# A fixed instruction order exchanged for another, with w_in's low parts made by TensorE, single VectorE steps and a split accumulator

## The chip, the cores and the metric

The kernel runs on one core of a Trainium2 chip. Its engines are TensorE (PE; PEld is its weight load), VectorE (DVE), ScalarE (ACT), GpSimd (POOL) and SyncE (SP), which here issues the loads and stores. The metric is the device time of one execution in microseconds (us).

## The reference

A gated linear attention (4 batches, 8 heads, 768 steps, head size 48) feeds a feed-forward layer (3072 tokens, 384 to 2048 to 384).

```python
for t in range(S):
    state = alpha[:, :, t, :, None] * state + np.einsum('bhd,bhe->bhde', k[:, :, t], v[:, :, t])
    y[:, :, t] = np.einsum('bhd,bhde->bhe', q[:, :, t], state)
x = np.ascontiguousarray(y.transpose(0, 2, 1, 3)).reshape(B * S, H * D)
h = x @ w_in
sp = np.maximum(h, 0.0) + np.log1p(np.exp(-np.abs(h)))
g = h * erf(sp)
return (g @ w_out).astype(np.float32)
```

The weights arrive as 64-bit floats; q, k, v and alpha as 32-bit floats.

## The kernel before

**Attention** goes in 24 chunks (2 pairs of batches, 12 chunks of 64 steps). A chunk n has these steps, each a method of `Chunk`: loads `la lk lq lv` (SP); `sb`, a scan over alpha backwards with the reciprocal of its segment ends and their copy into `start`, and `sa`, the scan forwards (DVE); `kk`, `qq`, the scaled K and Q (DVE); `pn`, four transposes of K (PE), and `kn`, their eviction (ACT); `td`, the decayed state (DVE); `qt`, `ps`, `sv`, `pu`, small matrix products that occupy parts of the PE array (lines 333 to 384), named by their outputs py, pS, py and pu; `mk`, the causal mask (DVE); `ta`, the new state (DVE); `xh` (ACT) and `xl` (DVE), the output split into a high part and a rest.

**The feed-forward layer** goes in 12 block rows (0 to 11) of 256 tokens (two chunks each), a block row in 4 groups g of 512 hidden features, a group in two halves. Steps, methods of `Moe`: `hm`, 18 matmuls of 128x256 (three products of high and low parts over three K tiles) into `ph`; `he`, its eviction to `hs` (ACT); `u`, tanh (ACT); `n1`, `n2`, `n3`, two logarithms and an exponential (ACT); `m1`, two chained DVE steps (t from s and w, then w from t and w); `g`, a Gelu (ACT); `z1`, `z2` (DVE); per half `ga`, the high part gh (ACT), `gl`, the rest gl (DVE), and `om`, 18 matmuls into the accumulator `acc`; at the end of a block row `oe` (ACT) and `od` (SP), three outputs each. `u` and `g` need another ACT table set than `n1` to `n3`; `need` loads it where it changes (line 225). A *block* below means one `hm` or one `om`: 192 in all; a *block row* is the 256 tokens that share an accumulator.

**The weights** come in 12 chunks of w_in (`wli` loads, n = 3g + K tile) and 16 of w_out (`wlo`). Each is turned into 32-bit floats by `wy` (ACT), `wv` and `wz` (DVE: a shift, then two chained bitwise steps on `wbuf`), then split: `wh` the high part (ACT), `wq` the low part (DVE subtract). Group g of `hm` needs chunks 3g to 3g + 2 of w_in.

**The order** is one table, ORDER (line 26): step names in sequence. Each instruction of PE, DVE, ACT and SP is issued through a `Queue` (line 168) that ties it to the one before it on its engine, so every engine works strictly in the table's order and waits where its next step isn't ready. All of them have line 176 in the profile. Behind the table come eight small DVE steps and one matmul that test whether values stayed in range, and a branch to a general version that isn't taken.

Of the kernel before, what the change touches and what calls it, by code (L numbers as in the profile page):

```python
# [10 lines left out]
F32 = mybir.dt.float32  # L11
# [8 lines left out]
RMAX = 1e30  # L20
# [6 lines left out]
wli_5 wyi_5 wvi_5 la_0 sb_0 wzi_5 whi_5 sa_0 wli_9 wyi_9 lk_0 kk_0 pn_0 wqi_5 kn_0 wvi_9 lq_0 qq_0 ps_0 wzi_9  # L27
mk_0 wli_8 wyi_8 wvi_8 lv_0 sv_0 whi_9 wqi_9 la_1 wlo_7 wzi_8 wli_1 wli_2 sb_1 whi_8 wqi_8 sa_1 wli_4 wyi_2
wvi_2 xh_0 lk_1 xl_0 wyi_1 wzi_2 whi_2 wlo_0 wlo_6 wvi_1 wli_0 pu_0 ta_0 lq_1 wzi_1 td_1 la_2 whi_1 wyi_4 qq_1
kk_1 wqi_2 pn_1 kn_1 wvi_4 lk_2 wlo_3 qt_1 ps_1 wli_3 wqi_1 sb_2 wzi_4 whi_4 sa_2 mk_1 wyi_0 wvi_0 kk_2 wyo_7  # L30
wvo_7 lv_1 wlo_1 sv_1 xh_1 wzi_0 whi_0 wzo_7 pu_1 ta_1 wyo_1 wqi_4 wli_7 wyi_7 wvo_1 xl_1 wqi_0 pn_2 td_2 wvi_7
wli_11 who_7 wzo_1 wzi_7 wyi_3 lv_2 wvi_3 wqo_7 wzi_3 hm_0_0_0 he_0_0_0 hm_0_0_1 lq_2 wyo_0 wvo_0 qq_2 wli_6
lk_3 who_1 wqo_1 he_0_0_1 wli_10 u_0_0 wzo_0 who_0 la_3 sb_3 wyo_6 wlo_4 wvo_6 sa_3 kn_2 qt_2 wzo_6 whi_3 whi_7
wqi_7 n1_0_0 wyi_6 wqi_3 wyo_3 ps_2 mk_2 wlo_2 wqo_0 sv_2 wvi_6 n2_0_0 n3_0_0 xh_2 hm_0_1_0 he_0_1_0 wvo_3 who_6
pu_2 wzi_6 whi_6 kk_3 lv_3 m1_0_0 g_0_0 wqo_6 hm_0_1_1 wzo_3 wqi_6 ta_2 z1_0_0 wyi_10 wvi_10 z2_0_0 he_0_1_1
hm_0_2_0 he_0_2_0 wyi_11 xl_2 pn_3 kn_3 wzi_10 wvi_11 wlo_15 who_3 wqo_3 td_3 lq_3 qq_3 lk_4 wlo_5 whi_10 wzi_11
wqi_10 wyo_4 wvo_4 hm_0_2_1 wlo_8 qt_3 ps_3 whi_11 mk_3 wyo_2 wvo_2 sv_3 wqi_11 hm_0_3_0 lv_5 he_0_2_1 ga_0_0_0
wlo_11 gl_0_0_0 wyo_15 wvo_15 u_0_2 wzo_4 xh_3 xl_3 u_0_1 wzo_15 ga_0_0_1 gl_0_0_1 wzo_2 he_0_3_0 who_4 wqo_4
who_15 la_4 sb_4 n1_0_2 pu_3 ta_3 wyo_5 wqo_15 hm_1_0_0 he_1_0_0 n1_0_1 hm_0_3_1 he_0_3_1 wvo_5 kk_4 who_2 wzo_5
om_0_0_0 n2_0_1 n3_0_1 lv_4 hm_1_2_0 lq_4 he_1_2_0 sa_4 wqo_2 pn_4 om_0_0_1 qq_4 td_4 qt_4 n2_0_2 wyo_8 m1_0_1  # L40
wvo_8 n3_0_2 m1_0_2 g_0_1 wlo_9 hm_1_3_0 he_1_3_0 z1_0_1 g_0_2 wzo_8 z2_0_1 z1_0_2 kn_4 hm_1_0_1 he_1_0_1 who_5
wqo_5 lq_5 la_5 ga_0_1_1 gl_0_1_1 ga_0_1_0 gl_0_1_0 wlo_10 z2_0_2 hm_1_3_1 he_1_3_1 wyo_10 wvo_10 wyo_11 wvo_11
who_8 wyo_9 wvo_9 hm_1_2_1 ps_4 wqo_8 wlo_14 wlo_12 lk_5 hm_1_1_0 u_0_3 he_1_2_1 om_0_1_0 mk_4 wzo_11 pu_4 u_1_0
n1_1_0 wzo_9 sv_4 who_11 wzo_10 sb_5 om_0_1_1 who_10 wqo_10 who_9 sa_5 hm_1_1_1 xh_4 xl_4 ta_4 wyo_14 n1_0_3
kk_5 n2_0_3 wvo_14 pn_5 td_5 qq_5 n3_0_3 ga_0_2_1 gl_0_2_1 qt_5 wqo_11 om_0_2_1 kn_5 m1_0_3 u_1_2 wzo_14 wlo_13
wyo_12 ps_5 mk_5 sv_5 pu_5 wqo_9 ga_0_2_0 gl_0_2_0 om_0_2_0 he_1_1_0 wvo_12 lk_6 he_1_1_1 who_14 g_0_3 z1_0_3
wyo_13 lq_6 la_6 xh_5 xl_5 u_1_1 n1_1_1 z2_0_3 ga_0_3_0 wzo_12 who_12 wqo_14 ga_0_3_1 sb_6 hm_2_0_0 he_2_0_0
n2_1_0 gl_0_3_1 hm_2_2_0 he_2_2_0 gl_0_3_0 wvo_13 n3_1_0 n1_1_2 ta_5 hm_2_0_1 hm_2_3_0 wzo_13 om_0_3_1 who_13
n2_1_2 he_2_0_1 m1_1_0 n3_1_2 g_1_0 he_2_3_0 lv_6 wqo_13 u_2_0 wqo_12 om_0_3_0 lv_7 oe_0_1 od_0_1 hm_2_2_1 kk_6
m1_1_2 g_1_2 oe_0_2 z1_1_0 pn_6 sa_6 he_2_2_1 kn_6 la_7 hm_2_3_1 z2_1_0 ga_1_0_1 ga_1_0_0 oe_0_0 qq_6 lk_7 td_6  # L50
# [36 lines left out]
u_7_0 m1_6_1 lk_17 gl_5_2_1 la_17 gl_5_2_0 u_6_3 pn_16 qt_16 kn_16 he_7_2_0 om_5_2_1 om_5_2_0 ga_6_0_1 m1_6_2
# [44 lines left out]
def gla_moe(ctx: ExitStack, tc: tile.TileContext, q, k, v, alpha, w_in, w_out, out):  # L132
# [652 lines left out]
```

## Time and profile before

| | us |
|---|---|
| median of 3 runs (lowest, highest) | 566.34 (564.23, 567.69) |
| the profiled execution | 565.46 |
| its span, first to last instruction | 563.7 |
| PE busy / DVE busy / ACT busy | 512.1 / 487.3 / 472.3 |
| last accumulator matmul ends | 556.3 |

Busy time counts an instruction's own record. Records of one engine overlap a little where the next needn't wait: the start-to-start distance in a full queue, called the *slot* below, is shorter than the record. A matmul's record is longer still than its slot.

### The profile page before, as it was taken

To read this page: it belongs to the slowest core of one execution; us is meant where nothing else is said; L and a number is where in the kernel's file an instruction comes from. 1 tells how busy PE (TensorE), PEld (TensorE's weight loads), DVE (VectorE), ACT (ScalarE), POOL (GpSimd) and SP (SyncE) were. 2 spreads that over 40 slices of the span, in tenths; PEclk is the share of its full clock that TensorE was granted. 3 is DMA by queue.
4 is the path that set the end of the run, shared out by engine and by line. 5 is a ranking of instruction groups with operands and counts; after the bars stand their busy time and mean duration, and the time that the engine had idled before them with its cause. 6 is when DMAs were issued, how large, how long until landed. Compare 5 with 4: busy or idle time off the path is not lost.

```text
span 563.7 us, 17947 instructions
## 1 busy us (share of the span) xinstructions
PE 512.1 (91%) x7962; PEld 491.4 (87%) x7962; DVE 487.3 (86%) x649; ACT 472.3 (84%) x644; POOL 3.5 (1%) x18
## 2 busy tenths in 40 slices
PE   0255899989999999999999999999999999999894
PEld 0245789989999999999999999999999999999884
DVE  6899999999989999979698798989787988676972
ACT  2337799989999999999988979989988998999961
POOL 2000000000000000000000000000000000000000
PEclk9998989989999999999999999999999999999988
DMA  6986232321302221113103112113110111000001
GB/s 182 279 266 189 91 104 86 91 63 54 82 15 68 72 49 48 59 30 99 28 10 110 34 44 76 31 42 102 44 57 22 49 49 44 2 10 20 2 29 34
DMA packets 38101, 38.98 MB, mean 69 GB/s; under 512 B 22144, under 2 KB 26752, under 8 KB 38016
## 3 DMA queue, kind: packets, MB, share of 16 engines
q1 hardware_dynamic: 38016, 37.76, 23.3%
q8 instruction: 64, 1.05, 0.8%
q14 instruction: 21, 0.17, 0.1%
HBM read 33.03 MB, written 4.72 MB: 67 GB/s over the span
## 4 chain that ended last, share of the span: by engine, by line
PE 76%; DVE 10%; ACT 7%; issue 3%; DMA 2%; SPq 0%; ACTq 0%; DVEq 0%
PE ph L176 33%; PE acc L176 32%; PE py L176 5%; DVE wbuf L176 3%; PE pS L176 2%; ACT s L176 2%; PE pu L176 2%; DMA raw_a<-in_alpha_dram 2%; ACT w L176 2%; PE pn L176 2%; ACT L176 1%; ACT gh L176 1%; DVE wi_lo L176 1%; DVE B L176 1%; DVE gl L176 1%
## 5 line engine op out<-in xcount | busy, mean ns | idle before, releaser
L176 PE MATMUL acc<-gh,wo_hi 128*128 128x256 f32 x576 | 167.1, 290 | 2.0 <-ACT o L176 2.0
L176 PE MATMUL ph<-x_hi,wi_hi 128*128 128x256 f32 x576 | 167.9, 292 | 0.0
L176 PE MATMUL acc<-gl,wo_hi 128*128 128x256 f32 x576 | 163.5, 284 | 1.2 <-DVE gl L176 1.0
L176 PE MATMUL ph<-x_lo,wi_hi 128*128 128x256 f32 x576 | 163.8, 284 | 0.0
L176 PE MATMUL ph<-x_hi,wi_lo 128*128 128x256 f32 x576 | 163.5, 284 | 0.2 <-DVE wi_lo L176 0.2
L176 PE MATMUL acc<-gh,wo_lo 128*128 128x256 f32 x576 | 163.0, 283 | 0.0
L176 PEld LDWEIGHTS acc<-gh,wo_hi 128*128 128x128 f32 x576 | 109.8, 191 | 4.8 <-ACT o L176 2.2
L176 PEld LDWEIGHTS ph<-x_hi,wi_hi 128*128 128x128 f32 x576 | 110.4, 192 | 2.5 <-issue 0.3
L176 PEld LDWEIGHTS acc<-gl,wo_hi 128*128 128x128 f32 x576 | 109.9, 191 | 2.2 <-DVE gl L176 2.2
L176 PEld LDWEIGHTS ph<-x_hi,wi_lo 128*128 128x128 f32 x576 | 110.3, 192 | 0.7 <-DVE wi_lo L176 0.7
L176 PEld LDWEIGHTS ph<-x_lo,wi_hi 128*128 128x128 f32 x576 | 110.4, 192 | 0.3 <-DVE x_lo L176 0.3
L176 PEld LDWEIGHTS acc<-gh,wo_lo 128*128 128x128 f32 x576 | 109.8, 191 | 0.0
L176 DVE TENSOR_TENSOR gl<-hs,gh 128x512 fp32r<-128x512 f32 x96 | 65.0, 686 | 24.0 <-ACT gh L176 23.8
L176 ACT ACTIVATE hs<-ph 128x512 f32<-128x512 f32 x96 | 56.2, 589 | 22.6 <-PE ph L176 22.3
L176 ACT ACTIVATE gh<-hs 128x512 fp32r<-128x512 f32 x96 | 59.5, 625 | 17.0 <-PE acc L176 11.9
L176 ACT ACT_TABLE_LOAD x50 | 64.2, 1283 | 1.6 <-PEq L745 0.8
L176 DVE TENSOR_TENSOR s<-s,w 128x1024 f32<-128x1024 f32 x48 | 58.2, 1219 | 8.4 <-ACT s L176 8.4
L176 DVE TENSOR_TENSOR t<-s,w 128x1024 f32<-128x1024 f32 x48 | 58.6, 1220 | 6.1 <-ACT w L176 5.6
L176 DVE SCALAR_TENSOR_TENSOR w<-t,w 128x1024 f32<-128x1024 f32 x48 | 58.8, 1225 | 1.6
L176 DVE SCALAR_TENSOR_TENSOR hs<-s,hs 128x1024 f32<-128x1024 f32 x48 | 58.0, 1219 | 0.6
L176 ACT ACTIVATE s<-s,fixed 128x1024 f32<-128x1024 f32 x48 | 54.6, 1148 | 0.3
L176 ACT ACTIVATE s<-hs 128x1024 f32<-128x1024 f32 x48 | 50.5, 1059 | 1.3 <-DVE wbuf L176 0.8
(61 smaller groups left out, 610.6 us busy)
## 6 DMA issues: line engine op xcount, KB each, us to landing
wst<-in_moe_w_in_dram SPq DMA_DIRECT2D x12, 512.0 KB, 6.9
raw_v<-in_v_dram SPq DMA_DIRECT2D x24, 256.0 KB, 3.3
wst<-in_moe_w_out_dram SPq DMA_DIRECT2D x16, 384.0 KB, 3.5
raw_a<-in_alpha_dram SPq DMA_DIRECT2D x48, 96.0 KB, 2.9
raw_k<-in_k_dram SPq DMA_DIRECT2D x48, 96.0 KB, 2.5
raw_q<-in_q_dram SPq DMA_DIRECT2D x48, 96.0 KB, 2.3
out_dram<-o SPq DMA_DIRECT2D x36, 128.0 KB, 2.0
```

The costliest lines, as they stand in the source:

```text
L176: ins = made(*args, **kw)
```

## The change

- ORDER is another table. In it `qt` and `ps` of a chunk mostly stand side by side on PE, and so do `sv` and `pu`: the 92 small-product steps stand in 71 uninterrupted runs before and in 47 now.
- w_in's low parts: `wp` (PE) adds the chunk times the identity, in 32-bit floats, and the high part times minus the identity, into a PSUM tile `rest` of the pool that `ph` uses; `we` (ACT) copies it out. `wq` on DVE stays for w_out alone.
- `wz` becomes `wa` and `wb`, `m1` becomes `ma` and `mb`, and `sb` gives its reciprocal to `rc`, so that other DVE steps can stand between. `rc` writes `start` itself, and `ic` (ACT) copies it into `inv`, which was the other way round and on DVE.
- The accumulator is two PSUM tiles (outputs 0 and 1; output 2) where it was one.
- The range test is three steps of the table, ahead of the last two output evictions, and the last output's store is issued by ACT.
- `u`/`g` and `n1` to `n3` alternate more often: 50 table loads are executed before, 64 now (counted in the order).

```diff
 ORDER = """
-wli_5 wyi_5 wvi_5 la_0 sb_0 wzi_5 whi_5 sa_0 wli_9 wyi_9 lk_0 kk_0 pn_0 wqi_5 kn_0 wvi_9 lq_0 qq_0 ps_0 wzi_9
+wli_0 wyi_0 wvi_0 wai_0 la_0 sb_0 rc_0 wli_7 wbi_0 whi_0 wpi_0 wli_9 lk_0 sa_0 wyi_7 wvi_7 wai_7 wyi_9 wli_5
...
+    act.activation(minus, ident, AF.Copy, scale=-1.0)
...
-            dve.reciprocal(inv[:, self.n, :], self.B[:, 1 : 1 + L : SEG])
-            dve.tensor_copy(out=start[:, 0:L:SEG], in_=inv[:, self.n, :])
+
+        def rc(self):
+            dve.reciprocal(start[:, 0:L:SEG], self.B[:, 1 : 1 + L : SEG])
+
+        def ic(self):
+            act.activation(inv[:, self.n, :], start[:, 0:L:SEG], AF.Copy)
...
-        def m1(self, g):
+        def ma(self, g):
             self.t = self.pl.tmp.tile([P, GT * TB], F32, name="t", tag="tmp")
             dve.tensor_tensor(out=self.t, in0=self.s[g], in1=self.w[g], op=ALU.mult)
+
+        def mb(self, g):
             w = self.w[g]
...
-                self.acc = self.pl.acc.tile([P, 2, 512], F32, name="acc", tag="acc")
+                self.acc = [self.pl.acc.tile([P, 512], F32, name="acc", tag=f"acc{n}") for n in range(2)]
...
+        def wp(self):
+            self.rest = ps_h.tile([P, 512], F32, name="rest", tag="h")
+            o = self.rest[:, : self.n]
+            pe.matmul(out=o, lhsT=ident, rhs=self.z, start=True, stop=False)
+            pe.matmul(out=o, lhsT=minus, rhs=self.hi, start=False, stop=True)
+
+        def we(self):
+            act.activation(self.lo, self.rest[:, : self.n], AF.Copy)
```

PE, around the products of chunk 14 (py<-Q,T is `qt`, pS is `ps`; ph and acc are rows of 18-matmul blocks). Before:

```order
L176 MATMUL ph<-x_hi,wi_lo 128x256
L176 MATMUL py<-Q,T 32x64 x32
L176 MATMUL ph<-x_hi,wi_hi 128x256
...
L176 MATMUL acc<-gl,wo_hi 128x256
L176 MATMUL pS<-Q,K 64x64 x16
L176 MATMUL ph<-x_hi,wi_hi 128x256
```

and in the change:

```order
L185 MATMUL acc<-gh,wo_lo 128x256
L185 MATMUL acc<-gl,wo_hi 128x256
L185 MATMUL py<-Q,T 32x64 x32
L185 MATMUL pS<-Q,K 64x64 x16
L185 MATMUL acc<-gh,wo_hi 128x256
```

The two products were islands of their own between blocks, two blocks apart; now they follow each other.

ACT, from the first eviction of a hidden-layer block (hs<-ph) to the second table load. Before:

```order
L176 ACTIVATE hs<-ph 128x512
L176 ACT_TABLE_LOAD
L176 ACTIVATE s<-hs 128x1024
L176 ACTIVATE wo_hi<-wbuf 128x384
L176 ACTIVATE wbuf<-wst 128x384
L176 ACTIVATE kn<-pn 128x512
L176 ACTIVATE wi_hi<-wbuf 128x512 x2
L176 ACT_TABLE_LOAD
L176 ACTIVATE s<-s,fixed 128x1024
```

and in the change:

```order
L185 ACTIVATE hs<-ph 128x512
L185 ACTIVATE wbuf<-wst 128x512
L185 ACTIVATE wi_lo<-rest 128x512
L185 ACTIVATE wo_hi<-wbuf 128x384
L185 ACT_TABLE_LOAD
L185 ACTIVATE s<-hs 128x1024
L185 ACTIVATE wbuf<-wst 128x384
L185 ACTIVATE wi_hi<-wbuf 128x512
L185 ACTIVATE hs<-ph 128x512
L185 ACT_TABLE_LOAD
L185 ACTIVATE s<-s,fixed 128x1024
```

The evictions wi_lo<-rest are new on ACT, and a block's eviction now stands between the two table loads.

DVE, the start of its queue behind the memsets. Before:

```order
L176 TENSOR_SCALAR wbuf<-wst 128x512
L176 SCALAR_TENSOR_TENSOR B<-raw_a,back 128x520
L176 RECIPROCAL inv<-B 128x8
L176 COPY start<-inv 128x8
L176 SCALAR_TENSOR_TENSOR wbuf<-wbuf 128x512 x2
L176 SCALAR_TENSOR_TENSOR A<-raw_a,start 128x520
L176 TENSOR_TENSOR K<-raw_k,B 128x512
L176 TENSOR_TENSOR wi_lo<-wbuf,wi_hi 128x512
```

and in the change:

```order
L185 TENSOR_SCALAR wbuf<-wst 128x512
L185 SCALAR_TENSOR_TENSOR wbuf<-wbuf 128x512
L185 SCALAR_TENSOR_TENSOR B<-raw_a,back 128x520
L185 RECIPROCAL start<-B 128x8
L185 SCALAR_TENSOR_TENSOR wbuf<-wbuf 128x512
L185 SCALAR_TENSOR_TENSOR A<-raw_a,start 128x520
```

The copy and the subtract wi_lo are gone, and the two bitwise steps on wbuf stand apart.

## Rows read from the trace of the kernel before

**Rows 1.** The page: the 40 slices of the span (busy tenths of PE, DVE, ACT).

```profile
PE   0255899989999999999999999999999999999894
...
DVE  6899999999989999979698798989787988676972
ACT  2337799989999999999988979989988998999961
```

**Rows 2.** Stretches of the span: us, busy us and instructions of PE, PEld, DVE, ACT, POOL, then the granted clock, the DMA share and GB/s.

```profile
0.00:20.00 20.00, 4.44 (x132) 3.55 (x132) 14.03 (x26) 5.88 (x9) 3.49 (x18) 1.00 0.75 224
20.00:40.00 20.00, 6.06 (x199) 5.10 (x200) 18.27 (x33) 6.95 (x15) 0.00 (x0) 1.00 0.83 255
...
440.00:500.00 60.00, 60.00 (x970) 57.68 (x969) 48.22 (x59) 54.67 (x71) 0.00 (x0) 1.00 0.09 27
```

**Rows 3.** PE in order of time (start us, us, what): the end of a block, small products, the start of the next; py alone, pS alone, py and pS together.

```profile
269.51 0.27 PE L176 MATMUL ph<-x_hi,wi_lo 128*128 128x256 f32 x1
269.71 0.86 PE L176 MATMUL py<-Q,T 48*32 48x64 f32 x64
...
270.72 0.28 PE L176 MATMUL ph<-x_lo,wi_hi 128*128 128x256 f32 x1
...
256.01 0.28 PE L176 MATMUL ph<-x_hi,wi_lo 128*128 128x256 f32 x1
256.22 0.70 PE L176 MATMUL pS<-Q,K 48*64 48x64 f32 x32
...
257.07 0.28 PE L176 MATMUL ph<-x_lo,wi_hi 128*128 128x256 f32 x1
...
138.14 0.28 PE L176 MATMUL ph<-x_hi,wi_lo 128*128 128x256 f32 x1
138.34 0.86 PE L176 MATMUL py<-Q,T 48*32 48x64 f32 x64
...
139.98 0.28 PE L176 MATMUL acc<-gh,wo_lo 128*128 128x256 f32 x1
```

**Rows 4.** The chain that ended last, in order of time (start us, us, what): the four transposes of a chunk and one block, at full clock; then the group of pS (its 16 instructions of a chunk are 32 in the trace).

```profile
145.87 0.44 PE pn L176 x4
146.31 2.13 PE ph L176 x18
...
L176 PE MATMUL pS<-Q,K 48*64 48x64 f32 x768 | 17.9, 236 | 3.9 <-ACT kn L176 3.9
```

**Rows 5.** DVE in order of time where PE stops waiting, and PE's blocks there, the first of them at half clock.

```profile
115.97 0.69 DVE L176 TENSOR_TENSOR gl<-hs,gh 128x512 fp32r<-128x512 f32 x1
116.57 0.35 DVE L176 TENSOR_SCALAR wbuf<-wst 128x384 int32<-128x384 int32 x1
...
117.39 0.58 PE L176 MATMUL acc<-gh,wo_hi 128*128 128x256 f32 x1
117.77 0.41 PE L176 MATMUL acc<-gh,wo_lo 128*128 128x256 f32 x1
117.98 0.42 PE L176 MATMUL acc<-gl,wo_hi 128*128 128x256 f32 x1
...
120.77 0.28 PE L176 MATMUL ph<-x_hi,wi_hi 128*128 128x256 f32 x1
```

**Rows 6.** Groups by line: DVE (busy us, mean ns of one, idle before).

```profile
L176 DVE SCALAR_TENSOR_TENSOR w<-t,w 128x1024 f32<-128x1024 f32 x48 | 58.8, 1225 | 1.6
L176 DVE SCALAR_TENSOR_TENSOR wbuf<-wbuf 128x384 int32<-128x384 int32 (+1 forms) x56 | 33.9, 611 | 1.0
L176 DVE TENSOR_TENSOR gl<-hs,gh 128x512 fp32r<-128x512 f32 x96 | 65.0, 686 | 24.0 <-ACT gh L176 23.8
L176 DVE TENSOR_TENSOR wi_lo<-wbuf,wi_hi 128x512 fp32r<-128x512 f32 x12 | 8.1, 684 | 0.0
L176 DVE COPY start<-inv 128x8 f32<-128x8 f32 x24 | 4.2, 176 | 0.8
```

**Rows 7.** Groups by line: ACT.

```profile
L176 ACT ACT_TABLE_LOAD x50 | 64.2, 1283 | 1.6 <-PEq L745 0.8
L176 ACT ACTIVATE gh<-hs 128x512 fp32r<-128x512 f32 x96 | 59.5, 625 | 17.0 <-PE acc L176 11.9 <-DVE hs L176 4.7
L176 ACT ACTIVATE hs<-ph 128x512 f32<-128x512 f32 x96 | 56.2, 589 | 22.6 <-PE ph L176 22.3
L176 ACT ACTIVATION_READ_ACCUMULATOR x_hi<-py 128x1 f32 x24 | 4.7, 195 | 0.0
```

**Rows 8.** ACT in order of time: the first eviction of a hidden-layer block; a table switch; the last rows.

```profile
45.12 0.60 ACT L176 ACTIVATE hs<-ph 128x512 f32<-128x512 f32 x1 [3.11 <-PE ph L176]
...
500.25 1.05 ACT L176 ACTIVATE w<-w 128x1024 f32<-128x1024 f32 x1
501.32 1.28 ACT L176 ACT_TABLE_LOAD   x1
502.61 1.06 ACT L176 ACTIVATE s<-s 128x1024 f32<-128x1024 f32 x1
503.58 0.58 ACT L176 ACTIVATE hs<-ph 128x512 f32<-128x512 f32 x1
...
556.36 0.94 ACT L176 ACTIVATE o<-acc 128x256 f32<-128x256 f32 x3 [3.77 <-PE acc L176]
```

**Rows 9.** PE in order of time: its waits of over 0.15 us behind 121 us, and its last block.

```profile
520.74 0.39 PE L176 MATMUL acc<-gl,wo_hi 128*128 128x256 f32 x1 [0.20 <-DVE gl L176]
535.96 0.39 PE L176 MATMUL acc<-gh,wo_hi 128*128 128x256 f32 x1 [2.00 <-ACT o L176]
536.71 0.58 PE L176 MATMUL acc<-gl,wo_hi 128*128 128x256 f32 x1 [0.25 <-DVE gl L176]
545.09 0.39 PE L176 MATMUL acc<-gl,wo_hi 128*128 128x256 f32 x1 [0.34 <-DVE gl L176]
547.70 0.38 PE L176 MATMUL acc<-gl,wo_hi 128*128 128x256 f32 x1 [0.21 <-DVE gl L176]
...
556.05 0.27 PE L176 MATMUL acc<-gl,wo_hi 128*128 128x256 f32 x1
```

More of the change, by code (lines that the diff above doesn't have):

```diff
@@ L201, in gla_moe @@
         )
+    minus = const.tile([P, P], F32R, name="minus")
     fixed = const.tile([P, 2], F32, name="fixed")
@@ L237, in gla_moe @@
     PIECES = (((0, 0),), ((1, 16),), ((0, 32), (1, -16)))
[L238 removed]
+    ATTENTION = "la lk lq lv sb rc ic sa kk qq pn kn td qt ps mk sv pu ta xh xl".split()
     class Chunk:
@@ L684, in general @@
                         m.he(g, half)
-                    for step in (m.u, m.n1, m.n2, m.n3, m.m1, m.g, m.z1, m.z2):
+                    for step in (m.u, m.n1, m.n2, m.n3, m.ma, m.mb, m.g, m.z1, m.z2):
                         step(g)
@@ L700, in gla_moe, with f1, f2, f3 @@
         m.order = [tuple(arg[1:]) for name, arg in steps if name == "om" and arg[0] == n]
+    class Flags:
+        def f1(self):
+            bad = at.tile([P, L], F32, name="bad", tag="A", bufs=1)[:, : 2 * NS * NSEG]
+            bad = bad.rearrange("p (a n) -> p a n", a=2)
+            good = self.good = const.tile([P, 4], F32, name="good")
+            size = inv.rearrange("p n s -> p (n s)")
+            for k, (lim, op) in enumerate(((RMAX, ALU.is_le), (-RMAX, ALU.is_ge))):
+                dve.tensor_scalar(out=bad[:, k], in0=size, scalar1=lim, scalar2=None, op0=op)
+            dve.tensor_reduce(
+                out=good[:, 0:1], in_=bad.rearrange("p a n -> p (a n)"), op=ALU.min, axis=mybir.AxisListType.X
+            )
+            for k, (lim, op) in enumerate(((XMAX, ALU.is_le), (-XMAX, ALU.is_ge))):
+                dve.tensor_scalar(out=bad[:, 0, k * NS : (k + 1) * NS], in0=sums, scalar1=lim, scalar2=None, op0=op)
+            dve.tensor_reduce(out=good[:, 1:2], in_=bad[:, 0, : 2 * NS], op=ALU.min, axis=mybir.AxisListType.X)
+            dve.tensor_tensor(out=good[:, 2:3], in0=good[:, 0:1], in1=good[:, 1:2], op=ALU.mult)
+            dve.tensor_scalar(
+                out=good[:, 3:4], in0=good[:, 2:3], scalar1=-1.0, scalar2=1.0, op0=ALU.mult, op1=ALU.add
+            )
+        def f2(self):
+            self.pf = ps_at.tile([P, 2, 512], F32, name="pf", tag="b")
+            pe.matmul(out=self.pf[:1, 0, :1], lhsT=self.good[:, 3:4], rhs=ones, start=True, stop=True)
+        def f3(self):
+            self.total = const.tile([1, 1], I32, name="total")
+            dve.tensor_copy(out=self.total, in_=self.pf[:1, 0, :1])
+    flags = Flags()
     for name, arg in steps:
```

266 lines of the change are left out of this document (134 added, 132 removed).

## The prediction

> **What bounds the kernel now.** First the slices of the whole span [rows 1]: PE climbs over 80 us, then is at nines up to the last slices; DVE is full from the second slice on, long before PE is. Then the stretches [rows 2]: from 20 to 40 us DVE is busy 18.3 of 20 us and PE 6.1; from 440 to 500 us PE is busy all 60. Then PE's own waits [rows 9]: behind 121 us there are five, of 3.0 us together, none before 520 us. So there are three stages: a start that DVE sets, a middle of 400 us in which PE alone sets the time and waits for nobody, and a tail of short waits.
>
> The middle gives exact prices for PE. A block takes 2.13 us, four transposes 0.44 [rows 4]. A small product between blocks is priced from the start of the matmul before it to the start of the second one after it, less two block slots of 0.118: py 270.72 - 269.51 - 0.24 = 0.97, pS 0.82 (pu is taken like it), py and pS side by side 1.60 [rows 3]. Separately they would be 1.79, so standing together saves 0.19: one passage from the small products into a block and back is spared.
>
> PE's work before is then 192 x 2.13 + 46 x 0.97 + 46 x 0.82 + 22 x 0.44 - 21 joins x 0.19 = 497.0 us. Its last matmul ends at 556.3 [rows 9], so PE lost 59.3 us. I call real time less the work ahead in an engine's queue its *lag*. At the first block of block row 2 (120.77 us [rows 5], with 67.6 us of PE work ahead) PE's lag is 53.2. So 53.2 us were lost in the start and 6.1 in the tail.
>
> What set the 53.2 is seen just before [rows 5]: gl ends at 116.66 and the block that needs it starts at 117.39. The DVE slots ahead of that gl (half 0 of group 2 of block row 0), in the order of the queue: weights 26 wv, 52 wz, 12 + 13 wq, 47.9 us; attention of six chunks 34.4; the feed-forward steps 20.0; in all 102.3. A slot is the mean record less 0.08, as gl's record is 0.69 and the next starts 0.60 behind [rows 5], and 0.03 more than the record where the next reads its result; the means are those of [rows 6]. So DVE's lag is 14.3 and PE's 14.3 + (102.3 - 65.5 of PE work ahead) + some 0.7. **The lead of DVE's queue over PE's, 36.8 us, is the start's price.**
>
> **The change part by part.**
>
> *PE's work.* Joins: 92 steps in 47 runs are 45 joins, 24 more than before: 24 x 0.19 = -4.6 us, nearly all in the stage where PE sets the time. By the Trainium skill (TensorEngine Tiling (Array Packing), Key Properties) every change of tiling mode drains TensorE; py and pS are tiled differently (32 and 64 columns), so by it a join would save nothing and the sum be 4.6 higher. The rows show 0.19 saved at just such a passage.
> wp: 12 times. No row has it. Four transposes of 128 columns of 32-bit floats take 0.44, so 512 columns 0.44; products of such floats are recorded twice (pS [rows 4]), so 0.88; minus-identity 2 x 0.118. Between 0.66 and 1.1 at full clock, and about twice that at half clock, where a matmul's slot is 0.21 instead of 0.118 [rows 5]. I take 1.1, as pS is the nearer kind: +13.2, most of it ahead of the first hidden-layer block, where PE is busy 6 of 20 us. PE's work after: 497.0 - 4.6 + 13.2 = 505.6.
>
> *DVE's lead.* wq of w_in goes: 12 x 0.60 = 7.2 us of DVE [rows 6], all in the start. The copies go: 24 x about 0.1 (8 in the start, under 1 us). Splitting chains: where another step stands between, each spares some 0.11; 48 + 28 pairs, at most 8 us of DVE over the run, a third of it in the start. The rest is order: hidden-layer blocks of block row 1 come earlier on PE, weight and feed-forward steps later on DVE. Counting the changed queue with the same slots, the largest lead of DVE over PE at any om is 9.9 us: at half 1 of group 0 of block row 1, 111.6 us of DVE (weights 42.0, attention 40.3, feed-forward 29.4) against 101.7 of PE. At the other om of the first two block rows it is 4 to 9. DVE's lag itself is taken as 10 to 16: before it was 14.3; the loads bound it from below, since the last piece of w_in group 1 needs 8.06 MB in SP's new queue, which 224 and 255 GB/s [rows 2] bring by 34 us, when DVE has 26.6 us of work ahead of it (lag 8), and rc now also waits for the ACT copy ic of the chunk before, with all later scans and gl behind it. So by DVE PE's lag is 20 to 27.
>
> *PE's own start.* The first hidden-layer block has 17.5 us of PE work ahead (10 wp). It needs x_lo of chunk 1, 26.3 us into DVE's queue: at lag 10 that is 37 us; with every wp at half clock, up to 43. Lag 20 to 26.
>
> *ACT.* New on it: 14 table loads, 1.29 each from start to start [rows 8], 18.1 us; 12 we, like hs<-ph, 0.59 with a slot of 0.5, 6.0; 24 ic, no row: between nothing beside other work and 0.59, I take the 0.20 of the accumulator's read, 4.8 [rows 7]. Together 29 us on 472. ACT's queue reaches its largest lead over PE at group 2 of block row 1: 112.1 against 113.8, -1.7. Its lag at the first hidden-layer eviction (19.6 us into its queue, at 40 to 46 us) is 20 to 26; before, from the first such eviction at 45.1 us [rows 8] to 123 us it lost another 11 us to waits. So by ACT PE's lag is 20 to 36 (gh and gl behind it add 1.2).
>
> All three lines meet between 20 and 36. With three full engines in fixed order for some 130 us, waits add up rather than hide: **I take 29**, against 53.2 before.
>
> *Tail.* From the last hidden-layer block the changed order leaves 8 blocks, 17.0 us, against this chain: two evictions 1.1, u 1.0, gh 0.5, table and n1 2.3, gh 0.5, n2 1.0, gh 0.5, n3 1.0, ma, mb, z1, z2 5.0, gh and gl 1.3, two blocks 4.3: 18.5. PE loses at least 1.5 us; before it lost 6.1. I take 4. The split accumulator is worth at most the one wait on an output eviction, 2.0 us [rows 9], and is in this figure. The range test costs nothing: it stands behind the last gl, beside PE's last block, as before; without that cover 2 us. Behind the last matmul 7.3 us remain; a second store queue may spare 0.3.
>
> Sum: 505.6 + 29 + 4 + 7.0 = 545.6 span; the profiled execution is 1.8 over its span, the median 0.9 over that: **548 us**.
>
> **The rivals.**
>
> *Forecast*, 541 to 558: 0.66.
>
> *All lines meet low*: PE's lag 21, tail 2: 505.6 + 23 + 9.7 = 538 to 541. For it: PE ran 400 us without a wait on DVE that was nearly as full. 0.10.
>
> *Passages cost the same inside a run* as at its ends, so the joins save nothing: 553. So says the Trainium skill's rule on modes above. The row at 138 us speaks against it. 0.08.
>
> *ACT sets the start.* If ACT's lag at block row 1 is 45, as before, PE's is 45: 564, no change to speak of. Against it: ACT idled for DVE and PE then, whose work now comes earlier. The same would follow if a table switch cost more than 1.29: by the Trainium skill (ScalarE: Activation LUTs, What ACT_TABLE_LOAD costs) a drain makes it 2.66; 13 loads ahead of that om would raise ACT's line by 18 and give 565. The row shows the next activation starting 1.29 behind the load. 0.10.
>
> *Slower: ACT sets the whole run.* Its queue holds 454 us of slots before, 483 after; its last output starts at 556.4 [rows 8], so 103 us were waits. If they are handovers that recur rather than slack, ACT ends at 586 and the time is 596. It is slower from the point where over 79 of the 103 recur. Against it: from 440 to 500 us ACT was idle 5 of 60 us, PE 0, so there the waits are ACT's slack. 0.04.
>
> *It doesn't do what it says*: the rest tiles take their turn in ph's two buffers, so a late we holds up the next block; in the start alone, two of twelve stand among blocks: under 4 us, inside the range. 0.02.
>
> **Numbers.** A measurement can tell about 1% from no change: 560.7 to 572.0. Faster 0.87 (forecast, low, modes, part of the rest), same 0.09, slower 0.04. The range reaches from the low case to the upper end of ACT's line with a tail of 8: 505.6 + 36 + 8 + 9.7 = 559: 539 to 559.
>
> **What would show it.** PE's first hidden-layer block at 37 to 43 us; from some 60 us to the tail PE without waits; islands of 1.60; a table switch of 1.3; a span near 546. It would be wrong if PE shows waits on ACT (evictions, gh) between 60 and 200 us of over 10 us, or if wp takes over 2 us at full clock.

## The result

The changed kernel takes 546.03 us (median of 4 runs, 545.68 to 547.01) where the kernel before takes 566.4 (564.23 to 567.69): a ratio of 0.965, 95% interval 0.961 to 0.968. The forecast was 548, 539 to 559. The profiled execution took 547.01 us, the longest of the four, with a span of 545.3 (the forecast: 545.6).

### The profile page after: what moved, and what is told of

Read it like the earlier page. It is cut to its first block, busy times and chain, and to the rows that moved or that the text cites. A ratio compares the mean times of both kernels' runs of the same rounds, so it can differ in the third digit from the quotient of the medians.

```text
span 545.3 us, 18043 instructions
## 1 busy us (share of the span) xinstructions
PE 516.9 (95%) x7998; PEld 488.4 (90%) x7998; DVE 470.5 (86%) x613; ACT 496.2 (91%) x695; POOL 3.5 (1%) x18
## 3 DMA queue, kind: packets, MB, share of 16 engines
q8 instruction: 64, 1.05, 0.8%
## 4 chain that ended last, share of the span: by engine, by line
PE 52%; ACT 35%; DVE 6%; issue 4%; DMA 1%; DVEq 0%; ACTq 0%; SPq 0%
PE ph L185 22%; PE acc L185 20%; ACT s L185 10%; ACT w L185 6%; ACT L185 6%; ACT gh L185 4%; ACT hs L185 4%; PE py L185 3%; PE rest L185 2%; DVE wbuf L185 2%; PE pu L185 2%; PE pS L185 2%; PE pn L185 1%; DMA raw_a<-in_alpha_dram 1%; ACT kn L185 1%
## 5 line engine op out<-in xcount | busy, mean ns | idle before, releaser
L185 PE MATMUL ph<-x_hi,wi_hi 128*128 128x256 f32 x576 | 165.5, 287 | 1.0 <-ACT hs L185 0.9
L185 PE MATMUL acc<-gh,wo_hi 128*128 128x256 f32 x576 | 164.9, 286 | 0.4 <-ACT gh L185 0.3
L185 PE MATMUL ph<-x_lo,wi_hi 128*128 128x256 f32 x576 | 162.0, 281 | 0.2 <-DVE x_lo L185 0.2
L185 PE MATMUL ph<-x_hi,wi_lo 128*128 128x256 f32 x576 | 161.7, 281 | 0.0
L185 PEld LDWEIGHTS ph<-x_hi,wi_hi 128*128 128x128 f32 x576 | 108.5, 188 | 4.0 <-ACT hs L185 1.6
L185 PEld LDWEIGHTS acc<-gl,wo_hi 128*128 128x128 f32 x576 | 108.5, 188 | 3.6 <-DVE gl L185 3.5
L185 PEld LDWEIGHTS acc<-gh,wo_hi 128*128 128x128 f32 x576 | 108.5, 188 | 2.5 <-ACT gh L185 0.7
L185 PEld LDWEIGHTS ph<-x_lo,wi_hi 128*128 128x128 f32 x576 | 108.6, 188 | 0.5 <-DVE x_lo L185 0.4
L185 PEld LDWEIGHTS ph<-x_hi,wi_lo 128*128 128x128 f32 x576 | 108.5, 188 | 0.0
L185 DVE TENSOR_TENSOR gl<-hs,gh 128x512 fp32r<-128x512 f32 x96 | 65.3, 684 | 30.3 <-ACT gh L185 29.7
L185 ACT ACT_TABLE_LOAD x64 | 82.1, 1283 | 1.9 <-PEq L797 0.8
L185 DVE TENSOR_TENSOR t<-s,w 128x1024 f32<-128x1024 f32 x48 | 58.4, 1217 | 9.0 <-ACT w L185 8.7
L185 DVE SCALAR_TENSOR_TENSOR w<-t,w 128x1024 f32<-128x1024 f32 x48 | 58.4, 1218 | 0.6
L185 ACT ACTIVATE s<-s 128x1024 f32<-128x1024 f32 x48 | 50.3, 1057 | 2.2 <-DVE t L185 1.8
```

Source lines behind the costliest of these rows:

```text
L185: ins = made(*args, **kw)
```

## The profile after

First the page of the changed kernel: busy time of each engine, the 40 slices of PE, DVE and ACT, and the shares of the chain that ended last.

```profile
PE 516.9 (95%) x7998; PEld 488.4 (90%) x7998; DVE 470.5 (86%) x613; ACT 496.2 (91%) x695; POOL 3.5 (1%) x18
...
PE   1799999999999999999999999999999999999984
...
DVE  6899999999999999999698899698687887987772
ACT  3579999999999999898999999999899999999981
...
PE 52%; ACT 35%; DVE 6%; issue 4%; DMA 1%; DVEq 0%; ACTq 0%; SPq 0%
```

Against [rows 1] PE reaches its nines in the third slice instead of the sixth, and ACT reaches them in the fourth instead of the sixth. Then the stretches of the changed kernel (columns as in [rows 2]):

```profile
20.00:40.00 20.00, 16.77 (x353) 9.81 (x352) 18.57 (x35) 13.43 (x29) 0.00 (x0) 0.91 0.76 243
60.00:120.00 60.00, 58.81 (x1069) 56.28 (x1061) 58.10 (x92) 58.75 (x88) 0.00 (x0) 1.00 0.32 93
120.00:180.00 60.00, 59.82 (x1010) 57.35 (x1016) 57.46 (x70) 59.62 (x83) 0.00 (x0) 1.00 0.18 52
...
440.00:500.00 60.00, 59.43 (x800) 57.64 (x799) 50.84 (x56) 59.33 (x78) 0.00 (x0) 1.00 0.10 29
```

Between 20 and 40 us PE is busy 16.8 us where it was busy 6.1. From 60 us on PE has hardly an idle moment. But ACT has few either: 59.3 of 60 us at 440 to 500, where it had 54.7 [rows 2]. Two engines are full at once; what that means, the experiments tell.

PE of the changed kernel in order of time (start us, us, what, and in brackets the wait): the last low parts ahead of the first hidden-layer block, and PE's longest waits from 60 us on (four of 0.15 to 0.26 us are left out).

```profile
35.81 1.10 PE L185 MATMUL rest<-wbuf,ident 128*128 128x512 f32 x2 [0.48 <-DVE wbuf L185]
36.34 0.80 PE L185 MATMUL rest<-wi_hi,minus 128*128 128x512 f32 x1
36.98 1.02 PE L185 MATMUL rest<-wbuf,ident 128*128 128x512 f32 x2
...
38.07 1.02 PE L185 MATMUL rest<-wbuf,ident 128*128 128x512 f32 x2
...
39.28 0.39 PE L185 MATMUL ph<-x_hi,wi_hi 128*128 128x256 f32 x1
...
89.13 0.39 PE L185 MATMUL ph<-x_hi,wi_hi 128*128 128x256 f32 x1 [0.31 <-ACT hs L185]
...
110.37 0.39 PE L185 MATMUL ph<-x_hi,wi_hi 128*128 128x256 f32 x1 [0.63 <-ACT hs L185]
...
524.73 0.39 PE L185 MATMUL acc<-gl,wo_hi 128*128 128x256 f32 x1 [0.23 <-DVE gl L185]
529.32 0.39 PE L185 MATMUL acc<-gh,wo_hi 128*128 128x256 f32 x1 [0.31 <-ACT gh L185]
530.88 0.39 PE L185 MATMUL acc<-gl,wo_hi 128*128 128x256 f32 x1 [1.06 <-DVE gl L185]
533.48 0.38 PE L185 MATMUL acc<-gl,wo_hi 128*128 128x256 f32 x1 [0.22 <-DVE gl L185]
```

A wp costs 1.09 to 1.17 us from start to start at full clock. The first hidden-layer block starts at 39.28. Between 60 and 520 us PE waits six times, 1.8 us in all, 0.9 of it for ACT's evictions hs. The long wait for an output eviction of [rows 9], 2.00 us, is gone; the four waits of the tail come to 1.8 us.

Groups of the changed kernel that answer to [rows 6] and [rows 7], and two new ones (busy us, mean ns, idle before):

```profile
L185 DVE TENSOR_TENSOR gl<-hs,gh 128x512 fp32r<-128x512 f32 x96 | 65.3, 684 | 30.3 <-ACT gh L185 29.7
L185 ACT ACT_TABLE_LOAD x64 | 82.1, 1283 | 1.9 <-PEq L797 0.8
...
L185 ACT ACTIVATE hs<-ph 128x512 f32<-128x512 f32 x96 | 55.2, 587 | 1.7 <-PE ph L185 1.5
L185 ACT ACTIVATE wi_lo<-rest 128x512 fp32r<-128x512 f32 x12 | 7.1, 594 | 3.0 <-PE rest L185 2.9
L185 ACT ACTIVATE inv<-start 128x8 f32<-128x8 f32 x24 | 4.9, 204 | 0.0
```

ACT's evictions hs waited 22.3 us for PE before and 1.5 now, while DVE's gl waits 29.7 us for ACT's gh where it waited 23.8: ACT waits less, and DVE waits more for ACT.

## The experiments

Each kernel ran on one chip with the kernel before beside it. Ratios are to that; the changed kernel's is 0.965. Two different kernels are compared by their ratios, or in us where they ran on the same chip.

| kernel | us (lowest, highest) | ratio [95% interval] |
|---|---|---|
| the changed kernel without wp | 552.7 (551.2, 553.9) | 0.979 [0.976, 0.983] |
| wp alone | 572.1 (571.5, 572.7) | 1.014 [1.011, 1.017] |
| wp alone, we late | 573.5 (572.2, 575.2) | 1.017 [1.013, 1.020] |
| pairs chained | 556.9 (556.2, 557.2) | 0.986 [0.984, 0.988] |
| ic four times | 558.7 (557.8, 559.5) | 0.990 [0.987, 0.992] |
| ic on VectorE | 546.1 (545.5, 549.5) | 0.966 [0.963, 0.969] |
| runs split by blocks | 570.1 (568.4, 572.1) | 1.009 [1.006, 1.012] |
| runs split by pieces | 548.3 (548.0, 548.7) | 0.968 [0.966, 0.971] |
| wp twice | 554.5 (552.5, 557.3) | 0.984 [0.981, 0.988] |
| one accumulator | 547.5 (546.8, 548.6) | 0.967 [0.964, 0.970] |
| tail and two wq | 548.6 (547.2, 550.0) | 0.971 [0.969, 0.973] |
| the changed kernel again | 546.6 (545.1, 547.0) | 0.965 [0.962, 0.968] |

### The changed kernel without wp

Everything of the change but wp and we is in this kernel: the table, the single VectorE steps, ic and the split accumulator too.

```diff
-whi_0 wpi_0 wli_9
+whi_0 wli_9
...
-whi_7 wei_0 wpi_7 kn_0
+whi_7 wqi_0 kn_0
```

> The changed kernel's order, but w_in's low parts are again a VectorE subtract (wq, put where we stood), and wp and its products are gone. Theory A (the prediction's): the price of the start is the lead of VectorE's queue over TensorE's, plus VectorE's own lag of about 14 us. Counted with the prediction's slots, TensorE's work falls from 505.3 to 491.7 us and the largest lead rises from 9.9 to 30.7, so TensorE's lag at block row 1 should be 30.7 + 14 = 45 us and the time about 550 (548 to 553), some 4 us above the changed kernel's 546.0. Rival B (the removal of wq from VectorE is what buys the whole start, the order nothing): TensorE's lag stays at the 53 of the kernel before and the time is 557 to 560. Rival C (ScalarE alone sets the start of the changed kernel, and it loses 6 us of work here): TensorE's lag is not above 40 and the time is at or below 546.

Measured 552.7 us. PE of this kernel in order of time:

```profile
41.92 0.58 PE L178 MATMUL ph<-x_lo,wi_hi 128*128 128x256 f32 x1 [5.93 <-DVE x_lo L178]
...
116.41 0.39 PE L178 MATMUL ph<-x_hi,wi_hi 128*128 128x256 f32 x1 [0.60 <-ACT hs L178]
```

The first block begins earlier than in the changed kernel (at 35.41 us, not 39.28), and its second matmul waits 5.9 us for x_lo, which stands behind the returned subtracts in DVE's queue. The second row is the fourth hidden-layer block of block row 2; 71.8 us of PE work stand ahead of it, so PE's lag is 44.6, where theory A had 45 and rival B 53. So the rule by which the forecast priced the start gives the right number in the new order. Its path is not seen: the rule counts the lead at a gl, and PE waits for no gl here ahead of the tail; a lag of 42.5 stands at 73 us already, behind the waits for x_lo and for a w_in low part (1.9 us at 52.7). The change without wp is worth 2.1% of the 3.5%, and wp another 1.4% in this order.

### wp alone

```diff
-pn_0 wqi_5 kn_0
+pn_0 wpi_5 wei_5 kn_0
```

> The kernel before, with its order, only that each wq of w_in is replaced in its place by wp (TensorE) and, right behind it, we (ScalarE); everything else as before (chained steps, one accumulator; the scratch of the range test lies in another pool's memory, for room). Theory A: TensorE's work rises from 496.8 to 510.6 us, the largest lead of VectorE falls from 36.9 to 15.8, VectorE's lag stays 14.3, so TensorE's lag at block row 2 is 31 instead of 53.2 and the time is 555 to 559, 7 to 11 us below the kernel before. Rival B (the low parts buy the whole start): TensorE's lag falls to the changed kernel's 23 to 26 and the time is 549 to 552. Rival C (ScalarE, whose queue gets 6 us longer, holds its own line, which was 48 us late at the same place before): TensorE's lag is 42 or more and the time is 566 or above.

Measured 572.1 us: slower than the kernel before, by about 8 us. Theory A and rival B both failed, and rival C gave the time with another reason. Stretches of this kernel, and two of its waits up to 80 us (us in total, times, longest):

```profile
0.00:20.00 20.00, 6.06 (x106) 3.48 (x106) 11.58 (x21) 5.62 (x9) 3.49 (x18) 0.97 0.78 229
20.00:40.00 20.00, 13.52 (x240) 7.57 (x239) 16.66 (x30) 9.35 (x20) 0.00 (x0) 0.67 0.78 233
40.00:60.00 20.00, 15.59 (x213) 10.38 (x211) 15.08 (x31) 15.14 (x25) 0.00 (x0) 0.76 0.65 184
60.00:80.00 20.00, 17.38 (x277) 14.51 (x277) 15.04 (x24) 12.07 (x21) 0.00 (x0) 0.92 0.30 93
```

```profile
ACT wi_lo L172 <- PE rest L172: 15.7, 8, 4.0
...
DVE sT L172 <- PE pS L172: 8.5, 3, 4.1
```

DVE is busy 58.4 of the first 80 us here, and 71.3 before (the sum of the kernel before's same four stretches). It has less to do and finishes it no sooner, since its masks sT now wait for pS, which stands behind the wp in PE's queue; before, that wait was 0.2 us. The granted clock is 0.67 between 20 and 40 us, where the kernel before had 1.00 [rows 2]. At half clock a wp takes 2.30 us from start to start, twice its price at full clock:

```profile
39.44 2.08 PE L172 MATMUL rest<-wbuf,ident 128*128 128x512 f32 x2
...
41.74 1.59 PE L172 MATMUL rest<-wbuf,ident 128*128 128x512 f32 x2
```

PE's lag settles at 46 instead of 31.

### wp alone, we late

The same, with each we moved behind its wp as far as the two buffers allow.

```diff
-pn_0 wpi_5 wei_5 kn_0
+pn_0 wpi_5 kn_0
...
-whi_9 wpi_9
+whi_9 wei_5 wpi_9
```

> As the run with wp alone in the order of the kernel before, which took 572 us instead of the 555 to 559 expected, but each we stands just ahead of the next step that takes one of the two buffers (wp or hm), 1 to 25 steps behind its wp, where it stood directly behind it. Theory A2 (that run was slow because ScalarE stood 19 us waiting for wp's tile, and with it the evictions and VectorE's scores; the lead itself would have fallen): most of the 19 us go, VectorE's waits in the first 80 us shrink, and the time is 556 to 564. Rival B2 (TensorE is what is late: ten wp stand ahead of the first blocks at half clock, and each must wait in TensorE's queue for VectorE's wbuf and ScalarE's high part, whatever ScalarE does behind it): 568 to 573 again, TensorE's lag behind 125 us above 43.

Measured 573.5 us: rival B2. ACT's waits for rest shrink from 19.2 to 5.1 us (up to 125 us) and the time does not. So the place of we was not the cause. What is left is PE's queue: the products at half clock, and what stands behind them while they wait for wbuf and the high part. That is argued from what remains; neither of the two was tried by itself. That VectorE is relieved of 7.2 us is no gain by itself.

### Pairs chained again

```diff
-sb_7 ma_1_1 oe_0_0
+sb_7 ma_1_1 mb_1_1 oe_0_0
...
-sa_7 mb_1_1 td_7
+sa_7 td_7
```

> The changed kernel with mb directly behind ma and wb directly behind wa again (59 pairs of VectorE that stood apart), nothing else. Theory A: each chained pair costs some 0.11 us of VectorE, 6.5 us in all, a third of it ahead of 120 us, where VectorE's line is near: 0 to 2.5 us slower than the changed kernel. Rival (chaining changes which step is late, so that the order's gaps show): 4 us slower or more, with new waits for VectorE in TensorE's list.

Measured 556.9 us: the rival. 0.965 of the 564.9 that the kernel before took beside it would be 545.1, so this costs some 12 us, more than anything else that was taken out by itself (wp is worth 7.9). What the bare order is worth without split pairs and without wp was not tried. DVE's bitwise steps in order of time, of this kernel and then of the changed one, and between them the wait of this kernel's PE for gl:

```profile
119.73 1.15 DVE L179 SCALAR_TENSOR_TENSOR wbuf<-wbuf 128x384 int32<-128x384 int32 x2
120.80 0.69 DVE L179 TENSOR_TENSOR Q<-raw_q,A 128x512 f32<-128x512 f32 x1
```

```profile
PE acc L179 <- DVE gl L179: 7.0, 11, 1.1
```

```profile
114.63 0.55 DVE L185 SCALAR_TENSOR_TENSOR wbuf<-wbuf 128x384 int32<-128x384 int32 x1
115.10 0.69 DVE L185 TENSOR_TENSOR Q<-raw_q,A 128x512 f32<-128x512 f32 x1
```

The chained pair takes 1.07 us, two steps apart 2 x 0.47: 0.13 a pair, 59 pairs, under 8 us of DVE. That size was in the forecast. What was not: the second step of a pair, pulled forward, makes what stood between the two late, among it gl (7.0 us of PE's waits in 11 places; 1.7 in 4 in the changed kernel). That is about half of the loss: PE's steps are later than in the changed kernel by 2.6 us at the first hidden-layer block and by 5.5 at 101 us, with only 0.2 us of waits for gl up to there, but with one of 1.75 for hs at 93.1 and a granted clock of 0.91 between 80 and 100 us (1.00 in the changed kernel); they are 10.2 later at the last block. How much of it is DVE's time and how much what comes late was not tried apart.

### ic four times, and ic on VectorE

```diff
-            act.activation(inv[:, self.n, :], start[:, 0:L:SEG], AF.Copy)
+            for _ in range(4):
+                act.activation(inv[:, self.n, :], start[:, 0:L:SEG], AF.Copy)
```

> The changed kernel with each ic issued four times (the same copy), so ScalarE has 72 more instructions of 0.20 us, 14.4 us, 9.6 of them ahead of 213 us; nothing else. Theory A (from 41 to 213 us ScalarE has no gaps and is the line that TensorE's lag follows): 8 to 10 us slower than the changed kernel, 554 to 557. Rival C (three lines that stand within some us of each other, each with some slack): 2 to 5 us slower. Rival B (VectorE is the line, ScalarE's full look is waits that are slack): within 1 us.

Measured 558.7 us; 0.965 of the 564.9 that the kernel before took beside it would be 545.1, so 14.4 us of ACT cost some 13. No forecast reached that. PE's steps are later than in the changed kernel run again by 1.8 us at 95 us, 6.3 at 217 and 10.5 at 475 (the same small products compared in both traces): the loss doesn't stop at 213 us, as theory A had it, but runs on through the stage in which PE was thought to be alone.

```diff
-            act.activation(inv[:, self.n, :], start[:, 0:L:SEG], AF.Copy)
+            dve.tensor_copy(out=inv[:, self.n, :], in_=start[:, 0:L:SEG])
```

> The changed kernel with ic (the copy of the reciprocals into inv) on VectorE, directly behind rc, instead of on ScalarE. ScalarE loses 24 x 0.20 = 4.9 us, VectorE gains 24 times 0.1 to 0.18, 2.4 to 4.2 us. Theory A (ScalarE is the line that TensorE's lag follows from 41 to 213 us, where ScalarE has no gaps): the 16 ic of that stretch are 3.2 us, of which TensorE gets 1 to 2.5 back, so 543.5 to 545 where the changed kernel has 546. Rival B (VectorE's lead is the line, as in the kernel before): 1 to 3 us slower. Rival C (the three lines stand so near to each other that neither shows): within 1 us.

Measured 546.1 us beside 546.6 of the changed kernel on the same chip: no difference, rival C. Taken together: relieving ACT of 4.9 us (for 4.1 us of records more on DVE, 172 ns each) gains nothing that can be told, and loading it with 14.4 costs nearly all of it. That fits a kernel in which the lines of two engines cross; ACT was not relieved without loading DVE.

### Runs split: by whole blocks, and by pieces

```diff
-he_2_3_0 om_1_0_0 xl_6
+he_2_3_0 xl_6
...
-qt_7 ps_7
+qt_7 om_1_0_0 ps_7
```

> The changed kernel with its runs of small products split: from chunk 4 on, a whole block is moved between the two small products of a run wherever the order allows it (35 splits, 82 runs now where 47 stood); nothing else. Theory A (each join spares one passage of 0.19 us between small products and blocks): 35 x 0.19 = 6.6 us more of TensorE's work, and since TensorE works without waits there, the time rises by 5 to 7, to 551 to 553; islands of one product measure 0.8 and 1.0 us again. Rival (a passage costs the same inside a run as at its ends, so joining saves nothing): 546, within 1 us. A time above 553 would mean that the moved blocks make other engines late.

Measured 570.1 us. (The moved blocks join some other runs, so that 76 runs stand there, not 82.) The time is far above both theories, by the moved blocks: PE's waits in the whole run include

```profile
PE py L179 <- DVE T L179: 5.9, 3, 3.1
PE py L179 <- DVE sT L179: 5.5, 6, 1.1
PE py L179 <- DVE Q L179: 3.6, 4, 1.4
```

which the changed kernel has only in 1.7 us for sT. A product asked for one block too early waits. Behind three of these waits the granted clock is 0.83 (160 to 170, 180 to 190 and 230 to 240 us), where the changed kernel has 1.00. So this kernel prices a misplaced block, not a passage. The next one moves no step; om_1_0_0_1 issues the first 12 matmuls of the block and om_1_0_0_2 the other 6:

```diff
-he_2_3_0 om_1_0_0 xl_6
+he_2_3_0 om_1_0_0_1 xl_6
...
-qt_7 ps_7
+qt_7 om_1_0_0_2 ps_7
```

> The changed kernel, but in 18 of the runs of small products behind chunk 3 the last 6 of the 18 matmuls of the block that stands ahead of the run are held back and put between the two products. No step is moved, no work added; only TensorE passes 18 times more from small products into a block and back. Theory A (a join spares one passage of 0.19): 18 x 0.19 = 3.4 us above the changed kernel's time of this call, and islands of one product of 0.8 and 1.0 us in the trace instead of one of 1.60. Rival (a passage costs the same inside a run as at its ends): within 1 us of the changed kernel. The 24 us that the splitting by whole blocks cost would then be the moved blocks' waits for VectorE, of which this kernel has none.

Measured 548.3 us, 1.75 above the changed kernel's 546.6 on the same chip: half of what theory A had. PE in order of time, this kernel and the changed one run again, the same two products of chunk 14:

```profile
275.53 0.86 PE L181 MATMUL py<-Q,T 48*32 48x64 f32 x64
276.32 0.38 PE L181 MATMUL ph<-x_hi,wi_hi 128*128 128x256 f32 x1
...
277.22 0.69 PE L181 MATMUL pS<-Q,K 48*64 48x64 f32 x32
277.85 0.39 PE L181 MATMUL ph<-x_hi,wi_hi 128*128 128x256 f32 x1
```

```profile
275.19 0.86 PE L185 MATMUL py<-Q,T 48*32 48x64 f32 x64
275.98 0.69 PE L185 MATMUL pS<-Q,K 48*64 48x64 f32 x32
276.60 0.39 PE L185 MATMUL ph<-x_hi,wi_hi 128*128 128x256 f32 x1
```

From py to the end of pS it takes 277.85 - 275.53 = 2.32 us less six block slots of 0.118, 1.61, against 276.60 - 275.19 = 1.41: 0.20 for the passage. All islands of one product measure 0.98 and 0.82 here, those of both 1.61. So the passage is real at each of the 18 places, 3.5 us of work. Half of it reached the end. Where the rest went the trace shows in one place: the wait of pn at 83.4 us, 0.48 in the changed kernel, is 0.29 here, behind a split.

### wp twice

```diff
+            pe.matmul(out=o, lhsT=ident, rhs=self.z, start=True, stop=True)
             pe.matmul(out=o, lhsT=ident, rhs=self.z, start=True, stop=False)
```

> The changed kernel with the identity product of each wp done twice (the same result), so TensorE has 12 products of 128x512 32-bit floats more, by the trace some 0.8 to 0.9 us each at full clock: about 10 us. Theory A (ten of the twelve stand ahead of the first hidden-layer block, in which TensorE waits for VectorE and ScalarE anyway; only the last three in a row there, and the two among the blocks, are not covered): the first hidden-layer block starts 2 to 4 us later than the changed kernel's 39.3 and the time rises by 3 to 5, to 549 to 551. Rival (TensorE's own start sets the lag, all twelve are paid): +10, to 556. Other rival (the start is set by ScalarE and VectorE alone, so the products are all covered): within 1 us of 546 plus the 2 us of those among the blocks.

Measured 554.5 us, between theory A and the rival that all twelve are paid, and nearer to the rival; with an unusual spread (552.5 to 557.3). PE of its profiled execution, the shortest of the four, in order of time:

```profile
32.92 0.77 PE L185 MATMUL py<-sT,raw_v 64*32 64x64 f32 x55
36.67 0.32 PE L185 MATMUL py<-sT,raw_v 64*32 64x64 f32 x9 [2.98 <-issue]
```

The first hidden-layer block starts at 44.81, 5.5 us later: four products of 0.86 in a row (3.4) and a stop of 2.98 inside a small product, where the changed kernel waited 0.9 for sT. The stop has no releaser in the trace; it is taken up below. So the wp directly ahead of the first block are paid in full, and from the fourth block on every block starts 5.9 to 6.0 us late: PE's own start is one of the lines. The other three executions took 553.9, 555.1 and 557.3 us at a mean granted clock of 0.992, 0.991 and 0.988, the profiled one 552.5 at 0.997: the lower the clock, the longer. Where in the span that clock was lost they don't show.

### One accumulator; a version with another tail

```diff
-                self.acc = [self.pl.acc.tile([P, 512], F32, name="acc", tag=f"acc{n}") for n in range(2)]
+                self.acc = self.pl.acc.tile([P, 2, 512], F32, name="acc", tag="acc")
```

> The changed kernel with the accumulator in one tile again (outputs 0, 1 and 2 share it), nothing else. Theory A: the two tiles are worth at most the one wait for an output eviction that the kernel before shows, 2.0 us, and as the changed order puts other blocks between the evictions and the next block row, less: 0 to 1 us slower than the changed kernel. Rival (each of the eleven passages from one block row to the next waits for all three evictions once the tiles are one): 3 us slower or more.

Measured 547.5 us, 0.9 above the changed kernel, with intervals of the ratios that overlap; but five of its six runs are longer than every one of the changed kernel's six on the same chip. Of PE's waits only 0.3 us are for an output eviction. Two tiles are worth some 1 us at most, and that waits for evictions are the reason is not shown.

```diff
-... oe_11_2 od_11_2 f1 f2 f3 oe_11_0 oe_11_1 oa_11_1 od_11_0
+... f1 f2 f3 oe_11_0 od_11_0 oe_11_1 oa_11_1 oe_11_2 od_11_2
```

and wpi_4, wei_4, wpi_10, wei_10 replaced by wqi_4 and wqi_10 at the places of we.

> A version that may beat both kernels. In the last block row the evictions stand in the order 0, 1, 2 instead of 2, 0, 1: outputs 0 and 1 lie in an accumulator tile that the last block leaves 6 matmuls earlier, so two of the three evictions and stores no longer stand behind the last matmul; and the two wp that stand among the blocks (chunks 4 and 10) are VectorE subtracts again. Theory A: the tail gives 0.6 to 0.9 us, the two wp 2.3 us less of TensorE and 1.0 less of ScalarE against 1.2 more of VectorE, of which some 0 to 1 us comes through: 544.5 to 546 where the changed kernel has 546.3. Rival: VectorE's line is the nearest, so the 1.2 us cost as much as the tail gives: no change, 546 to 547.

Measured 548.6 us: slower than the changed kernel, its ratio's interval wholly above. Its first block starts 1.6 us later than the changed kernel's, about as far as the starts of the other runs lie apart (38.9 to 40.7 where nothing ahead of the first block was changed but an ic). Then PE waits once for a low part on VectorE:

```profile
PE ph L179 <- DVE wi_lo L179: 1.9, 1, 1.9
```

So two subtracts of 0.6 us cost PE a wait of 1.9, and the two products that they replace took 2.2. Behind that wait (at 50.4 us) the granted clock is 0.91 between 40 and 60 us, where the changed kernel has 1.00. And from the start of the last accumulator matmul to the end of the span it still takes 7.8 us: the evictions' order gave nothing. Why the median is higher by 2 to 3 us is not settled beyond these rows; the profiled execution, 550.0 us, is the longest of the five.

## Why the prediction came out as it did

**The bound and the rule for the start: the number right, the path only in part.** PE's lag at block row 2 was to fall from 53.2 to the twenties because DVE's lead falls from 36.8 to 9.9. It is 24.1 at the first block of block row 2 (103.1 us), 25.0 at the fourth hidden-layer block of it (110.37) and 26 at 167, and the change without wp, with a counted lead of 30.7, gives 44.6. But 21.8 of the 25 stand at the first hidden-layer block (39.28 us, with 17.5 of PE work ahead): that is the line of PE's own start, 20 to 26 in the forecast. And where the lead of 9.9 was counted, DVE follows PE. The gl of that block (half 1 of group 0 of block row 1), in the changed kernel and then with wp twice:

```profile
126.04 0.64 DVE L185 TENSOR_TENSOR gl<-hs,gh 128x512 fp32r<-128x512 f32 x1
```

```profile
131.99 0.65 DVE L185 TENSOR_TENSOR gl<-hs,gh 128x512 fp32r<-128x512 f32 x1
```

DVE has the same work ahead of it in both, and in both it ends 0.2 us before the block starts, though the second kernel's PE is 6 us later. So the lines meet, as the forecast said; that DVE's lead alone set the 25 is not shown. The rule has a condition that the forecast did not state: the leading engine must not wait for the follower. wp alone breaks it, and the rule was off by 15 us of lag there.

**Half clock: not in the sum but for wp.** The forecast's sum for the kernel before, 14.3 + 36.8 + 0.7, is 51.8 and not 53.2; the other 1.4 us arise behind 117.39 us, where PE's matmuls start 0.21 us apart [rows 5]. Over the span the granted clock was 0.982 before and is 0.995 now, which is 10 and 3 us of full-clock time not granted (an estimate: the missing share of each span). No run separates what the clock gave back from the shorter waits.

**wp, 1.1 each: right** (1.09 to 1.17). Treating it as a term of its own was wrong: with the old order the same edit costs 1.4%, with the new one it gains 1.4%. As far as these runs tell, it pays where the table lets wbuf, the high part and the tile be ready before each wp comes up.

**ACT's additions: right in size.** we 594 ns, ic 204 ns, 14 more table loads of 1283 ns. A table switch in the chain of the changed kernel:

```profile
516.02 1.28 ACT L185
517.32 1.06 ACT s L185
```

The next activation starts 1.30 behind the load. By the Trainium skill (ScalarE: Activation LUTs, What ACT_TABLE_LOAD costs) it would have been 2.66; the trace does not agree, and the rival built on that price is out.

**Joins, -4.6: right at the place, about half at the end.** The passage of 0.19 is shown by the islands. By the Trainium skill (TensorEngine Tiling (Array Packing), Key Properties) each change of tiling mode drains TensorE. The forecast took from this that a join of differently tiled products saves nothing, which does not follow: two islands between blocks hold four such changes, a joined run three. The 0.2 us saved at each join agree with one change less; what the change from py to pS inside a run costs no run here shows.

**PE's lag of 29, a tail loss of 4, 7.0 behind the last matmul: right in the sum, in part by luck.** With the forecast's slots, 486.5 us of PE work stand ahead of the last hidden-layer block, which starts at 515.4: a lag of 28.9. It grows to 32.0 at the last block, a tail loss of 3.1. The last matmul ends at 537.8, the span at 545.3, so 7.5 lie behind it. But 29 was not worked out: it was chosen between 20 and 36, and it was put on the start. 25 to 26 of it arise there; the other 3 come up in the middle, in steps of some tenths, where the forecast had no loss. And the median was put 0.9 above the profiled execution and came 1.0 below it, which makes most of the 2 us between 548 and 546.

**"From some 60 us to the tail PE alone": half wrong.** PE has hardly a wait there, 1.8 us in 460, as forecast. But ACT, whose waits were put down as slack, is as near: 14.4 us more of ACT lengthened the span by 11 and the median by 13. The rival "ACT sets the whole run", at 0.04, was nearer than its chance says: not in its own form, since the time is not 596, but ACT needs only a little more work to set it.

**Splitting the chains: mis-sized.** It was entered as DVE time, at most 8 us over the run and a third of that in the start; undone, it costs 12 us, about half of it behind waits for gl.

**Split accumulator, range test, second store queue: small, as forecast.** The accumulator is worth some 1 us at most. The range test and the store were not tried apart, but the 7.8 us behind the last matmul's start stand against 7.65 before, so the 0.3 us that the second store queue might have spared did not come.

## What to carry to other kernels

Price a start by the lead of one queue over another in program order, but first see whether the leading engine ever waits for the follower: where it does, work taken off it comes back as waits. Work moved to an idle engine paid here only in the order written for it, so try the edit and the order apart before crediting either. And when an engine that sets the pace has no waits, look how near the next one is by loading it a little: in this kernel moving 4.9 us from ACT to DVE gained nothing, and adding 14.4 us to ACT cost nearly their full time.

## What the runs showed of the hardware that was not expected

PE's stops without a releaser ("issue") inside a small product. In the changed kernel:

```profile
49.62 0.77 PE L185 MATMUL py<-sT,raw_v 64*32 64x64 f32 x55
51.37 0.32 PE L185 MATMUL py<-sT,raw_v 64*32 64x64 f32 x9 [0.97 <-issue]
```

In the six stops of 0.46 to 2.98 us that five of the traces show, the number of PE's records (matmuls, weight loads and 7 to 13 of its sequencer's) ahead of the stop is 449, 705 or 1217: 256 and 512 apart. All lie before 52 us, in stretches of 20 us in which the DMA share is 0.74 to 0.80. The page also lists a DMA queue for instructions with 64 transfers, 1.05 MB, 16 KB each; with wp twice, 48 of PE's records more, there are 65. In all six stops PE goes on 1.3 to 1.5 us after a transfer of that queue has landed (in the rows above at 51.37, after one that landed at 49.91). That PE waits there for its next piece of program, late behind the loads, fits all of this; no run tried it apart.
